# Linear attention and SwiGLU on one core: block 0's loads and order of work, and the shape of k by v

## The chip, the cores and the metric

The kernel runs on 1 core of one Trainium2 chip. The metric is the device time of one execution in microseconds (us), lower is better. Times are medians of several executions; one more execution was taken with the hardware profiler, and all rows of the profile are of that one.

## The reference

Two layers, one after the other, in float32 (the weights arrive as 64-bit words and are rounded in the kernel):

```python
kv  = einsum('bhsd,bhse->bhde', k, v)          # 8 batches, 8 heads, 576 positions, 64 wide
out = einsum('bhsd,bhde->bhse', q, kv)
rms = sqrt(mean(out * out, axis=-1, keepdims=True) + 1e-06)
x   = (out / rms * g_norm)                     # then (B,H,S,D) -> (B*S, H*D) = (4608, 512)

g   = x @ w_gate                               # 512 -> 1536
val = x @ w_val
y   = (g * sigmoid(g) * val) @ w_out           # 1536 -> 512
```

## The kernel before

The 4608 tokens are cut into 9 blocks of 512 (`BLK`), which don't coincide with the 8 batches of 576 positions. For every block n there is an `Att(n)` (attention, which yields the block's x, turned so that features lie on the partitions) and an `Ffn(n)` (the three weight products). `Att(n)` also makes the 64 by 64 matrices kv of batch n for all 8 heads, so block n needs kv of batches n - 1 and n. The later blocks' FFN uses a Strassen-like scheme with fewer products (`Up`, `Inner`, `Down`); while TensorE works on block n's FFN, attention of block n + 1 is fitted in between.

Block 0 is different: nothing runs beside it, and its FFN (`plain_up`, L956 to L961) goes through the 12 chunks f of 128 hidden features plainly, because the weights are just being loaded and rounded. Per weight piece (`Words`, 36 pieces: gate and value of each chunk, then the output weights) there is one DMA on SP (L135), two ScalarE (ACT) operations (L144 the low word, L146 the absolute value of the high word), and four VectorE (DVE) operations: L147 clamps, L152 takes the sign, L153 shifts and joins, L157 adds into the weight tile. Four load buffers (pool `ld`) go round, which the q tiles of block 0 use first.

The start of the kernel, as the code has it:

- `load_q(0)` (L268, SP): q tiles 0 and 1 of 128 positions, in pieces of 256 bytes.
- `load_kv(0)`, `load_kv(1)` (L229): per pair of heads j the 576 positions are shared out between the two halves of the partitions, 5 positions per partition (64 partitions by 5 = 320) in one and 4 (256) in the other, and the halves change places from pair to pair. That makes 8 DMAs for k (SP) and, in block 0 alone, 8 for v on ACT's queue, each on 64 partitions, 128 or 160 KB.
- `load_q(1)`: q tiles 2 and 3; `load_weights(4)`: the first four weight pieces.
- `first()`: `turn_q(0)` transposes q tiles 0 and 1 on TensorE (L307) into PSUM; the copies back go to DVE for tile 0 (L311) and ACT for the others (L309). `kv(0)`, `kv(1)` (L286) multiply k by v with 64 rows of contraction, for both halves of the partitions into two PSUM banks, which are then added: ACT copies one (L292), DVE adds the other (L111). `half(0)` is product 0 (L327, q by kv for tiles 0, 1), squares on ACT (L338), sums on DVE (L339), `root` (L345 to L357: eleven small DVE operations, a reciprocal square root by three Newton steps) and `scale` (L113). `turn_q(1)` and `product(1)` follow, and `turn_x(0)` transposes the first half of x (L374); ACT copies it back with the gain (L375).
- The main part then rounds the first two pieces, does chunk 0 for the first half of the tokens, and `second()`: root, scale and transposing of the second half. From chunk 2 on the products take all 512 tokens at once.

`tc.issue_after(ins)` orders what is traced under it behind `ins` on `ins`'s own engine; between engines only data (and buffers coming free) make one wait for another. Engines run their instructions in order, and each queue issues its DMAs in order.

In later blocks `load_kv` and `kv` work as above with all loads on SP: `kv(0)` after a third of the up products, `kv(1)` after two thirds; block 1's are done in the gap behind `plain_up`.

Of the kernel before, what the change touches and what calls it, by code (L numbers as in the profile page):

```python
# [14 lines left out]
P = 128  # L15
# [3 lines left out]
def kernel(  # L19
# [51 lines left out]
    NS = DM // P  # L71
    NF = FF // P
    NP = NF // 2
    KT = 5
    LD = 2 * (2 * KT - 1) * D
    eps = 1e-6
    assert NT == B * S and NT == NB * BLK and NB == B + 1 and S - BLK == BLK // B
    assert 2 * D == P and H == 2 * NS and (2 * KT - 1) * D == S and NS == 4

    def pool(name, bufs, **kw):  # L80
        return ctx.enter_context(tc.tile_pool(name=name, bufs=bufs, **kw))
# [37 lines left out]
    class Words:  # L119
# [12 lines left out]
        def __init__(self, src, shape):  # L132
            self.raw = ld_pool.tile([P, LD], U32, name="ld")[:, 0 : 2 * BLK]
            dst = self.raw.rearrange("p (a b) -> p a b", a=shape[0])
            self.sent = nc.sync.dma_start(out=dst, in_=src)  # L135
            self.shape = shape

        def round_to(self, dst):
            halves = self.raw.rearrange("p (f w) -> p f w", w=2)
            low, high = halves[:, :, 0], halves[:, :, 1]  # L140
            room = ring()

            unit = room[:, 0]
            nc.scalar.activation(out=unit, in_=low, func=ACT.Copy, scale=2.0**-51, bias=2.0)  # L144
            mag = room[:, 1].bitcast(U32)
            nc.scalar.activation(out=mag.bitcast(F32), in_=high.bitcast(F32), func=ACT.Abs)  # L146
            nc.vector.tensor_scalar(  # L147
                out=mag.bitcast(F32), in0=mag.bitcast(F32), scalar1=self.LOW, scalar2=self.HIGH,
                op0=OP.max, op1=OP.min,
            )  # L150
            sign = room[:, 2].bitcast(U32)
            nc.vector.tensor_scalar(out=sign, in0=high, scalar1=0x80000000, scalar2=None, op0=OP.bitwise_and)  # L152
            nc.vector.scalar_tensor_tensor(  # L153
                out=mag, in0=mag, scalar=3, in1=sign, op0=OP.logical_shift_left, op1=OP.bitwise_xor
            )
            a, b = self.shape[0], BLK // self.shape[0]
            nc.vector.tensor_tensor(  # L157
                out=dst.bitcast(U32),
                in0=mag.rearrange("p (a b) -> p a b", a=a, b=b),
                in1=unit.bitcast(U32).rearrange("p (a b) -> p a b", a=a, b=b),  # L160
                op=OP.add,
            )
# [15 lines left out]
    def round_w(name, j):  # L178
        if name == "o":
            dst = wo[:, j : j + 1, :]  # L180
        else:
            dst = wviews[name][0][j // 2][:, :, P * (j % 2) : P * (j % 2 + 1)]
        words.pop((name, j)).round_to(dst)

    class Att:

# [18 lines left out]

        def place_kv(self, g, i):

            n = (2 * g + i) * LD
            if self.n == 0:
                return self.room.rearrange("p f t -> p (f t)")[:, n : n + LD]  # L210
            if self.n == 1 and g == 0:
                return self.room[:, n : n + LD]
            return ld_pool.tile([P, LD], F32, name="ld")

        def load_kv(self, g):


            if self.n == B:
                return
            for i, (views, src) in enumerate(((self.k, k), (self.v, v))):  # L220
                tile_ = self.place_kv(g, i)
                for e in range(2):
                    j, s0 = 2 * g + e, 0
                    for r in range(2):
                        m = KT - (r != e)
                        at = 2 * D * (KT - r) * e
                        t = tile_[r * D : (r + 1) * D, at : at + 2 * D * m].rearrange("p (h x) -> p h x", h=2)
                        queue = nc.scalar if self.n == 0 and i else nc.sync
                        queue.dma_start(  # L229
                            out=t,  # L230
                            in_=src[self.n, 2 * j : 2 * j + 2, s0 : s0 + m * D].rearrange("h (p t) d -> p h (t d)", t=m),
                        )
                        views[j, r] = t.rearrange("p h (t d) -> p h t d", t=m)
                        s0 += m * D

        def load_quarters(self, i):

# [35 lines left out]
        def kv(self, g):  # L273


            if self.n == B:
                return
            if g == 0:
                self.kv_ps = [m_psum.tile([P, NS, D], F32, name="m") for _ in range(2)]
            for e in range(2):  # L280
                j = 2 * g + e
                for c in range(KT):
                    for r in range(2):
                        m = KT - (r != e)
                        for u in range(2 if c < m else 0):
                            nc.tensor.matmul(  # L286
                                self.kv_ps[r][u * D : (u + 1) * D, j, :], lhsT=self.k[j, r][:, u, c, :],
                                rhs=self.v[j, r][:, u, c, :], start=(c == 0), stop=(c == m - 1),
                            )
            if g == 1:  # L290
                dst = kvs[self.n % 3]
                nc.scalar.copy(out=dst, in_=self.kv_ps[0])  # L292
                self.kv_made = add(nc.vector, dst, self.kv_ps[1], dst)

        def turn_q(self, i, pools=None):

            if i == 0:
                self.qt = ring().rearrange("p j (t c) -> p t j c", t=T)
            if self.n >= TURNED:
                to = self.qt[:, :, 2 * i : 2 * i + 2].rearrange("p t j c -> p j t c")  # L300
                nc.vector.transpose(out=to.rearrange("p j t c -> p (j t c)"), in_=self.q[i])
                return
            for t in (2 * i, 2 * i + 1):
                pool = pools[t % 2] if pools else m_psum
                ps = pool.tile([P, NS, P], F32, name=pool.name[0])
                for j in range(NS):
                    nc.tensor.transpose(ps[:, j], self.q[t][:, j], ident)  # L307
                if t:
                    nc.scalar.copy(out=self.qt[:, t], in_=ps)  # L309
                else:  # L310
                    nc.vector.tensor_copy(out=self.qt[:, t], in_=ps)  # L311

        def product(self, i, pools=None):
# [7 lines left out]
            for t in range(2):  # L321
                for j in range(NS):
                    for b, _, p0, p1 in self.parts(2 * i + t):
                        for p in range(p0, p1, D):
                            for u in range(2):
                                rows = slice(u * D, (u + 1) * D)
                                nc.tensor.matmul(  # L327
                                    self.ps[i][u][p : p + D, t, j, :],
                                    lhsT=self.qt[rows, 2 * i + t, j, p : p + D], rhs=kvs[b % 3][rows, j, :],
                                    start=True, stop=True,  # L330
                                )
# [4 lines left out]
            for u in range(2):  # L336
                sq = self.sq[:, 2 * i + u]
                self.squared = nc.scalar.activation(out=sq, in_=self.ps[i][u], func=ACT.Square)  # L338
                nc.vector.tensor_reduce(out=self.z[:, i, u], in_=sq, axis=mybir.AxisListType.X, op=OP.add)  # L339

        def root(self, i, k=1):

# [84 lines left out]

        def first(self):
            self.turn_q(0, (b_psum, c_psum))
            for g in range(2):  # L430
                self.kv(g)
            self.half(0)
            squared = self.squared
            self.turn_q(1, (b_psum, c_psum))
            with tc.issue_after(self.scaled.ins):
                self.product(1, (b_psum, a_psum))
            self.turn_x(0)
            return squared, self.scaled

        def second(self):  # L440
            self.root(1)
            self.scale(1)
            self.turn_x(1)
            return self.scaled

        def turn(self):
            for i in range(2):
# [548 lines left out]
    blocks = [Att(n) for n in range(NB)]  # L996
    blocks[0].room = h_pool.tile([P, NF, BLK], F32, name="h")
    blocks[0].load_q(0)
    for g in range(2):
        blocks[0].load_kv(g)  # L1000
    blocks[0].load_q(1)
    load_weights(4)
    squared, scaled = blocks[0].first()
# [1 line left out]
    for n in range(NB):  # L1005
        ffn = Ffn(n, blocks[n])
        nxt = blocks[n + 1] if n + 1 < NB else None
        if n == 0:
# [1 line left out]
            with tc.issue_after(squared.ins), tc.issue_after(scaled.ins):  # L1010
                weights(2)
            ffn.plain_up(0, (0,))
            scaled = blocks[0].second()
            for f in range(NF):
                with tc.issue_after(scaled.ins), tc.issue_after(blocks[0].copied.ins) if f else ExitStack():
                    weights(2 * (f + 2))
                if f == 1:
                    ffn.plain_up(1, (0,))
                    ffn.plain_up(0, (1,))
                ffn.plain_up(f, (1,)) if f == 1 else ffn.plain_up(f) if f else None  # L1020
            weights(len(pieces))
            pairs = wo.rearrange("p (j e) d -> p e j d", e=2)
            t2(pairs[:, 0, :, HD:DM], pairs[:, 1, :, HD:DM], pairs[:, 0, :, 0:HD])
# [22 lines left out]
            ffn.up({4: third, 8: two_thirds} if nxt else {})  # L1046
        if nxt:
            nxt.turn()
        if n + 2 < NB:
            blocks[n + 2].load_kv(0)  # L1050
        if TURNED - 2 <= n < NB - 2:
            ffn.loads = blocks[n + 2].load_q
# [2 lines left out]
                    ffn.loads(i)  # L1055
        ffn.down(nxt)
        if n == 0:

            with tc.issue_after(nxt.halves[0].ins):
                for j in range(NP):  # L1060
# [32 lines left out]
```

## Time and profile before

| | |
|---|---|
| median of 5 runs | 1040.93 us (1039.65 to 1041.39) |
| the profiled execution | 1041.1 us, span in the profile 1039.3 us, mean granted clock 0.995 |
| L956, all of block 0's up product on TensorE | busy 36.0 + 36.0 + 9.8 + 7.8 us |
| L286, k by v of block 0 | 144 passes, median 311 ns; 936 of later blocks from the load buffers, median 218 ns |
| first and last L286 pass of block 0 | 7.81 and 16.3 us |
| DVE, in the stretch 80 to 109 us | busy 28.5 of 29 us |

The span is cut into rows of operations with their engine, line, tile, shape and time; start times are us from the span's start. A matmul of float32 appears as two passes, each with a load of its weights (PEld). "Idle before" names what ended an engine's wait. SPq and ACTq are the queues that issue DMAs; a DMA's issue is short, its landing comes 2 to 8 us later. POOL is GpSimd. Busy time of TensorE says that it has work, not that its clock is at full rate: that is the granted clock, a column of the tables of windows.

### The profile page before, as it was taken

What the parts mean: (1) busy time and instruction counts of PE and PEld (TensorE: products, weight loads), DVE (VectorE), ACT (ScalarE), POOL (GpSimd) and SP (SyncE); (2) the same over time, 40 slices, a digit from 0 to 9 for tenths busy, and PEclk for the clock granted to TensorE, in tenths of its full rate; (3) what the DMA queues carried; (4) which work ended last, traced back from release to release, by engine and by line L of the source; (5) the groups of instructions that cost most, each with busy time, mean ns of one, the idle gap of its engine ahead of it and who ended that gap; (6) DMA issues with size and microseconds to landing.
All of it is one profiled execution on the core that took longest, in us unless ns stands there. A gap on an engine that the chain in (4) does not pass through costs nothing.

```text
span 1039.3 us, 21544 instructions
## 1 busy us (share of the span) xinstructions
PE 1011.5 (97%) x8588; PEld 907.5 (87%) x8588; DVE 700.2 (67%) x1202; ACT 232.0 (22%) x357; POOL 368.9 (35%) x280
## 2 busy tenths in 40 slices
PE   4899999999999999999999999999999999999998
PEld 3644688778899989998999899988999899989997
DVE  2999596888656866675666666684668566856661
ACT  3666111222212111121111111211122111212110
POOL 0000443435024631563147305640455136512670
PEclk9899999999999999999999999999999999999999
DMA  9689604665457556764676377726862666066611
GB/s 213 189 257 274 151 1 126 186 196 142 129 179 242 134 108 196 242 161 82 196 239 190 60 203 229 218 48 172 249 194 52 162 207 188 29 153 210 191 31 41
DMA packets 255044, 168.16 MB, mean 162 GB/s; under 512 B 124640, under 2 KB 230240, under 8 KB 254944
## 3 DMA queue, kind: packets, MB, share of 16 engines
q1 hardware_dynamic: 228384, 162.45, 55.7%
q10 hardware_dynamic: 26496, 4.33, 2.4%
q8 instruction: 68, 1.11, 0.4%
q14 instruction: 32, 0.26, 0.1%
q0 software_dynamic: 64, 0.00, 0.0%
HBM read 138.02 MB, written 22.41 MB: 154 GB/s over the span
## 4 chain that ended last, share of the span: by engine, by line
PE 91%; DVE 4%; DMA 3%; issue 1%; ACT 1%; POOL 0%; SPq 0%; DVEq 0%; ACTq 0%; POOLq 0%
PE b L662 25%; PE b L513 20%; PE c L662 12%; PE c L513 9%; PE a L662 6%; PE a L513 5%; PE b L956 4%; PE c L956 4%; PE m L286 1%; PE m L327 1%; DVE xi L112 1%; DMA w<-t 1%; DVE r L111 1%; DVE r L112 1%; DMA h<-in_k_dram 1%
## 5 line engine op out<-in xcount | busy, mean ns | idle before, releaser
L111 POOL TENSOR_TENSOR r<-r 128x256 f32<-128x256 f32 (+1 forms) x105 | 110.8, 1061 | 308.9 <-DVE r L111 233.3
L111 DVE TENSOR_TENSOR r<-b,r 128x512 f32<-128x512 f32 (+1 forms) x273 | 161.9, 606 | 64.0 <-PE b L662 58.9
L112 POOL TENSOR_TENSOR t<-wo 128x512 f32<-128x512 f32 x81 | 115.2, 1447 | 195.4 <-DVE wo L111 106.7
L111 DVE TENSOR_TENSOR r<-c,r 128x512 f32<-128x512 f32 (+1 forms) x179 | 108.5, 618 | 88.9 <-PE c L662 49.5
L662 PE MATMUL b<-x,t 128*128 128x128 f32 x1092 | 151.0, 275 | 0.0
L662 PEld LDWEIGHTS b<-x,t 128*128 128x128 f32 x1092 | 136.5, 192 | 0.6 <-DVE r L111 0.2
L111 DVE TENSOR_TENSOR r<-a,r 128x512 f32<-128x512 f32 (+1 forms) x99 | 62.5, 631 | 110.3 <-PE a L513 65.8
L113 POOL TENSOR_TENSOR h<-r 128x1024 f32<-128x1024 f32 (+1 forms) x40 | 81.5, 2053 | 88.0 <-DVE r L111 73.7
L662 PE MATMUL c<-xi,t 128*128 128x128 f32 x840 | 112.2, 275 | 0.3 <-DVE xi L111 0.3
L662 PEld LDWEIGHTS c<-xi,t 128*128 128x128 f32 x840 | 102.8, 192 | 0.4 <-DVE xi L111 0.4
L513 PE MATMUL b<-wo,h 128*128 128x256 f32 x432 | 99.4, 382 | 0.1
L513 PE MATMUL b<-t,h 128*128 128x256 f32 x432 | 96.9, 381 | 0.0
L513 PEld LDWEIGHTS b<-t,h 128*128 128x128 f32 x432 | 81.3, 190 | 11.3 <-issue 0.2
L513 PEld LDWEIGHTS b<-wo,h 128*128 128x128 f32 x432 | 79.9, 190 | 12.7 <-DVE h L113 2.5
L676 ACT COPY r<-b 128x512 f32<-128x512 f32 x63 | 36.9, 586 | 212.7 <-PE b L662 205.9
L662 PE MATMUL b<-xi,t 128*128 128x128 f32 x588 | 79.7, 276 | 0.0
L662 PEld LDWEIGHTS b<-xi,t 128*128 128x128 f32 x588 | 72.4, 192 | 0.0
L662 PE MATMUL b<-x,wg 128*128 128x128 f32 x336 | 52.7, 279 | 0.2 <-DVE x L112 0.2
L662 PE MATMUL b<-x,wv 128*128 128x128 f32 x336 | 51.3, 275 | 0.0
L956 PE MATMUL b<-x,wg 128*128 128x512 f32 (+1 forms) x112 | 45.8, 552 | 3.5 <-ACT r L144 2.4
L513 PE MATMUL c<-t,s 128*128 128x256 f32 x216 | 48.3, 380 | 0.0
L513 PE MATMUL a<-wo,h 128*128 128x256 f32 x216 | 48.3, 379 | 0.0
(133 smaller groups left out, 1582.8 us busy)
## 6 DMA issues: line engine op xcount, KB each, us to landing
t<-w SPq DMA_DIRECT2D x336, 256.0 KB, 3.4
out_dram<-r SPq DMA_DIRECT2D x17, 512.0 KB, 3.1
ld<-in_moe_w_gate_dram SPq DMA_DIRECT2D x12, 512.0 KB, 4.7
ld<-in_moe_w_val_dram SPq DMA_DIRECT2D x12, 512.0 KB, 4.8
ld<-in_moe_w_out_dram SPq DMA_DIRECT2D x12, 512.0 KB, 4.6
w<-t SPq DMA_DIRECT2D x18, 256.0 KB, 2.5
w<-xi SPq DMA_DIRECT2D x12, 384.0 KB, 3.1
ld<-in_k_dram SPq DMA_DIRECT2D x26, 160.0 KB, 3.9
```

Of the source, the lines that this page charges most:

```text
L111: add = lambda e, o, a, b: e.tensor_tensor(out=o, in0=a, in1=b, op=OP.add)
L112: sub = lambda e, o, a, b: e.tensor_tensor(out=o, in0=a, in1=b, op=OP.subtract)
L113: mul = lambda e, o, a, b: e.tensor_tensor(out=o, in0=a, in1=b, op=OP.mult)
L286: nc.tensor.matmul(self.kv_ps[r][u * D : (u + 1) * D, j, :], lhsT=self.k[j, r][:, u, c, :], rhs=self.v[j, r][:, u, c, :], start=(c == 0), ...
L327: nc.tensor.matmul(self.ps[i][u][p : p + D, t, j, :], lhsT=self.qt[rows, 2 * i + t, j, p : p + D], rhs=kvs[b % 3][rows, j, :], start=True, ...
L513: nc.tensor.matmul(banks[e][:, e], lhsT=lhsT, rhs=rhs, start=first and i == 0 and (e == 0 or banks[0] is not banks[1]), stop=i == self.ste ...
L662: nc.tensor.matmul(ps[:, i, f], lhsT=self.weight(o, p, f), rhs=self.operand(o, p), start=first and (i, f) == (0, 0), stop=True, skip_group ...
L676: nc.scalar.copy(out=dst, in_=ps)
L956: nc.tensor.matmul(t, lhsT=w[f // 2][:, i, P * (f % 2) : P * (f % 2 + 1)], rhs=x[:, i, of], start=(i == 0), stop=(i == NS - 1),)
```

## The change

Block 0:

- k and v of positions 0 to 511 are loaded as 4 positions by 128 partitions, 4 heads to a DMA (512 KB, all on SP); the last 64 positions come in four small DMAs on ACT's queue, onto the half of the partitions that their heads use. `first_kv` multiplies them: per head 4 chunks for each half of the partitions and one chunk of the last 64 positions, 72 products as before.
- `first()` has another order: product 0 stands ahead of turning q tiles 2 and 3; their copies go to DVE (tile 2) and ACT (tile 3).
- Rounding of a weight piece is cut into `begin` (absolute value; the three DVE operations) and `finish` (low word; the last add). The first piece's `begin` stands between the sums of the first and the second half; the second half's squares and sums come behind it.
- One `root` serves both halves (twice as wide), then come the first half's scaling, the first piece's `finish`, the second half's scaling.
- `warm()`: seven products of 512 columns with the identity, whose output nobody reads, stand on TensorE behind product 1 and in front of transposing x.
- Chunk 1 is no longer cut into halves.

Later blocks: k and v of a pair of heads lie on one half of the partitions, 9 positions to a partition (64 by 9 = 576), 288 KB per DMA, half as many DMAs. Each PSUM bank then holds finished matrices for its heads; ACT copies the two banks, and DVE's add is gone. Block 2's first load is traced behind the down product of block 0 instead of ahead of it.

```diff
-        def round_to(self, dst):
+        def begin(self):
+            self.begun = True
...
+        def finish(self, dst):
+            unit = self.room[:, 0]
+            nc.scalar.activation(out=unit, in_=self.low, func=ACT.Copy, scale=2.0**-51, bias=2.0)
...
+        def load_first_kv(self):
+            room = self.room.rearrange("p f (h x) -> p (f h) x", h=2)
+            most = {"k": room[:, 0:H], "v": room[:, H : 2 * H]}
+            last = {x: room[:, 2 * H + i].rearrange("p (h d) -> p h d", d=D) for i, x in enumerate("kv")}
+            for g in range(2):
+                heads, rows = slice(NS * g, NS * (g + 1)), slice(D * g, D * (g + 1))
+                for x, src in (("k", k), ("v", v)):
+                    nc.sync.dma_start(
+                        out=most[x][:, heads], in_=src[0, heads, 0:BLK].rearrange("h (p t) d -> p h (t d)", t=T)
+                    )
+                    nc.scalar.dma_start(out=last[x][rows], in_=src[0, heads, BLK:S].rearrange("h p d -> p h d"))
...
+        def first_kv(self):
+            banks = [m_psum.tile([P, NS, D], F32, name="m") for _ in range(2)]
+            for j in range(NS):
+                g = j // 2
+                for c in range(T + 1):
+                    for r in range(2) if c < T else (g,):
+                        for u in range(2):
...
+            nc.scalar.copy(out=kvs[0], in_=banks[0])
+            add(nc.vector, kvs[0], banks[1], kvs[0])
...
-                for e in range(2):
-                    j, s0 = 2 * g + e, 0
-                    for r in range(2):
-                        m = KT - (r != e)
...
+                for r in range(2):
+                    j = 2 * g + r
+                    t = tile_[r * D : (r + 1) * D].rearrange("p (h x) -> p h x", h=2)
+                    nc.sync.dma_start(
+                        out=t, in_=src[self.n, 2 * j : 2 * j + 2].rearrange("h (p t) d -> p h (t d)", t=KT)
+                    )
...
             if g == 1:
-                dst = kvs[self.n % 3]
-                nc.scalar.copy(out=dst, in_=self.kv_ps[0])
-                self.kv_made = add(nc.vector, dst, self.kv_ps[1], dst)
+                dst = kvs[self.n % 3].rearrange("p (g r) d -> p r g d", r=2)
+                for r in range(2):
+                    nc.scalar.copy(out=dst[:, r], in_=self.kv_ps[r])
...
         def first(self):
             self.turn_q(0, (b_psum, c_psum))
-            for g in range(2):
-                self.kv(g)
-            self.half(0)
-            squared = self.squared
-            self.turn_q(1, (b_psum, c_psum))
-            with tc.issue_after(self.scaled.ins):
+            self.first_kv()
+            self.product(0)
+            with tc.issue_after(self.multiplied.ins):
+                self.turn_q(1, (b_psum, c_psum))
+            with tc.issue_after(self.copied_q.ins), tc.issue_after(self.summed.ins):
+                begun = words[pieces[0]].begin()
+            with tc.issue_after(begun.ins):
                 self.product(1, (b_psum, a_psum))
+            self.warm()
+            self.root(0, 2)
+            self.scale(0)
+            with tc.issue_after(self.squared.ins), tc.issue_after(self.scaled.ins):
+                weights(1)
             self.turn_x(0)
-            return squared, self.scaled
-
-        def second(self):
-            self.root(1)
             self.scale(1)
-            self.turn_x(1)
-            return self.scaled
+            return self.squared, self.scaled
+
+        def warm(self):
+            ps = c_psum.tile([P, NS, P], F32, name="c")
+            for _ in range(7):
+                nc.tensor.matmul(ps, lhsT=ident, rhs=self.qt[:, 3], start=True, stop=True)
...
-                if f == 1:
-                    ffn.plain_up(1, (0,))
-                    ffn.plain_up(0, (1,))
-                ffn.plain_up(f, (1,)) if f == 1 else ffn.plain_up(f) if f else None
+                ffn.plain_up(f) if f else ffn.plain_up(0, (1,))
```

## The prediction

> **What bounds the kernel now.** I read four views: the page's engine shares, TensorE's waits, a table of windows, and the timeline of the first 50 us.
>
> ```profile
> PE 1011.5 (97%) x8588; PEld 907.5 (87%) x8588; DVE 700.2 (67%) x1202; ACT 232.0 (22%) x357; POOL 368.9 (35%) x280
> ```
>
> ```profile
> PE m L286 <- DMA h<-in_k_dram: 9.7, 2, 7.8
> PE m L374 <- DVE r L113: 3.1, 1, 3.1
> PE b L956 <- ACT r L144: 2.4, 1, 2.4
> PE m L327 <- issue: 1.2, 1, 1.2
> ```
>
> TensorE (PE) is the bound at 97%. What it waits for (us in total, times, longest) lies nearly all in block 0, so a gain is an earlier start of its unbroken stream.
>
> ```profile
> 7.50:10.00 2.50, 0.87 (x10) 0.71 (x10) 0.00 (x0) 0.71 (x1) 0.00 (x0) 1.00 1.13 232
> 14.00:16.00 2.00, 2.00 (x94) 2.00 (x91) 0.00 (x0) 0.18 (x1) 0.00 (x0) 1.00 1.29 214
> 18.00:20.00 2.00, 0.84 (x37) 0.64 (x27) 0.69 (x1) 0.68 (x3) 0.00 (x0) 1.00 1.08 348
> 26.00:28.00 2.00, 0.42 (x2) 0.02 (x1) 2.00 (x7) 1.93 (x4) 0.00 (x0) 0.50 0.01 4
> 30.00:32.00 2.00, 2.00 (x7) 1.55 (x6) 1.68 (x11) 0.68 (x1) 0.00 (x0) 0.50 0.75 227
> 47.00:60.00 13.00, 13.00 (x32) 5.80 (x32) 12.43 (x27) 8.59 (x15) 0.00 (x0) 1.00 0.80 248
> ```
>
> Columns: stretch, its length, busy us of PE, weight load, DVE, ACT, POOL, then granted clock, DMA share, GB/s. Three rates matter: 232 GB/s while k and v come (64 partitions), 214 while the last q comes (256-byte packets), 348 while weights come (128 partitions, 1 KB packets). The clock is halved after PE's idle time, and from 47 on PE is never idle.
>
> ```profile
> 13.49 2.99 PE L286 MATMUL m<-h 64*64 64x64 f32 x114
> 17.33 1.02 PEld L327 LDWEIGHTS m<-kv,r 64*64 64x64 f32 x63 [0.17 <-DVE kv L111]
> 23.67 1.29 DVE L113 TENSOR_TENSOR r<-m,y 128x512 f32<-128x512 f32 x2
> 28.83 3.75 PE L956 MATMUL b<-x,wg 128*128 128x256 f32 x8 [2.41 <-ACT r L144]
> 32.38 1.94 PE L956 MATMUL c<-x,wv 128*128 128x256 f32 x8
> 37.43 1.99 PE L956 MATMUL b<-x,wg 128*128 128x256 f32 x8 [0.77 <-DVE wg L157]
> 47.03 3.60 PE L956 MATMUL b<-x,wg 128*128 128x512 f32 x8
> ```
>
> Two milestones: the first half's scaling (L113) ends at 24.96, and chunk 2 of the up product starts at 47.03. Between lie 22.07 us, of which chunks 0 and 1 need 13.7 (32 passes of 0.43, from the last row). The same 8 passes of 256 columns take 3.75 us at the low clock and 1.9 later.
>
> **The change, part by part.**
>
> *Loads of block 0.* Sixteen DMAs (eight k on SP, eight v on ACT) become four of 512 KB on 128 partitions (SP) and four of 64 KB in 256-byte packets (ACT). DMAs in flight share completion slots: in the trace SP's third k issue waits until ACT's first v has landed (4.90 us, issue at 4.92). In the changed kernel as built the second big k waits so for ACT's first small load; behind it on SP stand the second v, both late q and the weights. By 5.0 us 715 kB have come; at 232 GB/s that means a start at 1.9. Then q 0, 1 and the small loads, 786 kB at 214, take 3.7 us; the first big k and v, 1.05 MB at 348, 3.0 (8.6); the second pair 3.0 (11.6); q 2 1.2 (12.8), q 3 1.2 (14.0), first weights 1.5 (15.5). The upper bound for k, v is 232 GB/s, putting the second pair at 14.6. I take 348, the row with the same partitions and packet size. A 64 KB load and one q before the slot-waiting DMAs are within the first 786 kB, so they should be down near 5, while the first big pair still feeds the engines.
>
> The page "DMA: Bandwidth & Descriptors" of the Trainium skill (Why small descriptors are slow) counts about 3 bus cycles per packet beside one per 32 bytes: 8 of 11 useful at 256 bytes, 32 of 35 at 1 KB, so 0.80 of the speed. The rows give 214 against 348, 0.61; by the page the 786 kB would take 2.8 us instead of 3.7 and the forecast would be 0.9 lower; I keep the rows.
>
> *k by v on TensorE.* The 144 passes stay. L286 ran one per 26 ns (2.99 us by 114), L327 one per 16. The 72 passes of the second pair, after idle time, at 26: 1.9, to 13.5. From the end of these products (16.48) to the first of L327 were 0.85 us, ACT's copy and DVE's add, both kept: the first product starts at 14.35.
>
> *The order up to the scaling.* PE now does product 0 before it turns q 2 and q 3. Its 64 passes cost 1.0 at 16 ns (to 15.55 with the last's latency) or 1.7 at 26. Turning q 2 is 0.66 (1.11 as at 11.59, cold); its copy goes to DVE (0.6, L311's 0.69 less overlap) and stands there ahead of the sums, so a late q 2 holds all of DVE. Then on DVE two sums of L339 1.2, the first weights' three operations (26.06 to 27.4 in the trace: 1.27), two sums of the second half 1.2, one root for both halves (eleven operations, 2.3 as at 21.30 to 23.58; twice the width, between nothing and 1.9 if time doubled with it; I take 0.2), scaling 1.29. The weights' ACT half and the four squares, 0.6 each, run beside and finish first (18.0 and 19.3). Sum from 15.55, warm: 0.66 + 0.6 + 1.2 + 1.27 + 1.2 + 2.5 + 1.3 = 8.7, with waits 24.4. Cold: 25.5. I take 25.0 against 24.96 before: the earlier data pay for the work put in front.
>
> *What no longer lies behind the scaling.* Before, DVE did the second sums (1.27), the two first pieces, then a second root (2.9) and scaling (1.3), idled 1.03, and only then the next two pieces. Now, with S the scaling's end: weights finished 0.6, second scaling 1.2, second piece with two operations of the third in between 2.6: value weights ready at S + 4.45. PE: turning 0.5, ACT's x copy 0.65, gate half (8 by 0.215) over at S + 2.8; value half S + 4.45 to 6.15. ACT: two copies to S + 1.85, three weight steps 1.7, table load 1.28, Silu 0.35, one step 0.6, second half's copies from S + 5.85. PE: second half from S + 6.5, 3.44, over at S + 9.95; its weights are ready at S + 8.75. Chunk 1, 6.87: chunk 2 starts at S + 16.9. Its own pieces are done at S + 14.7 and 16.2, needed at 16.9 and 20.3. With S = 25.0 that is 41.9, and 47.03 - 41.9 = 5.1 us gained.
>
> *The filler.* Seven matmuls of 512 columns, 14 passes of 0.43, 6.0 us, stand on PE in front of turning x. After product 1 (17.4 to 18.0) they end at 24.0, before S = 24.4: hidden. In the cold case they start near 20 and end at 26.0, 0.5 after S. The reader sees why they are there: from 21.9 to 25.0 PE is idle and the clock is 0.50 from about 25.6 to 32.5; without them about 2.1 of the 5.1 would go (3.75 + 1.94 - 3.6).
>
> The page "TensorE: Matmul & The Clock Gate" (The HAM clock gate) speaks against a fixed filler: its 3.4 us window is free-running, so how many passes are slow varies from run to run. The low-clock stretch of 6.9 us is two such windows, which agrees; by the page an unlucky phase leaves up to 3.4 us at half rate, some 1.7 us lost, and the forecast would be that much higher at worst.
>
> *Behind 47 us.* DVE's rounding (nearly full from 26 to 109) moves up by the work that now precedes S, 6 to 7 us, so it stays ahead; POOL's first subtractions of the output weights (109.52) start right behind it; and the last multiply waits for PE (DVE idle 5.95 before 115.97). The shift is kept. *Later blocks:* the add (0.42, eight times) goes off DVE and ACT's 0.37 copy becomes two of, by the rows 0.37 for 256 and 0.59 for 512 columns, about 0.27; hidden by the 5.35 us of the first down product (119.98) between copy and use; uncovered, eight times 0.17, 1.4 us. Half as many loads of 128/160 KB become 288 KB, each 0.6 of SP; PE's waits for DMA behind 47 us are 0.5 in all, the most that this can gain. Loss bound from both, 1.4; I take nothing.
>
> The sum goes against the profiled execution: 1041.1 us, span 1039.3, 0.2 over the median 1040.93. 1041.1 - 5.1 = **1036.0**.
>
> **Rivals.**
> *Slow start:* k, v come at 232 as before, or instruction fetch stalls PE 1.16 us again (the "issue" wait in L327, at about the same count of instructions, which is now the turning of q 2), or the filler runs partly cold. For it: these rows were all measured here; against it: 128-partition rows at 348. Gain 5.1 - 3.0 = 2.1: 1039.0; the stall alone 1037.2.
> *Fast start:* PE is warm throughout and both pairs overlap; second products at 16 ns (0.75 less), S at 23.6: gain 6.5, 1034.6.
> *Hidden anyway:* rounding, not PE, paces 47 to 109, where DVE is 12.43 of 13 busy; then the gain is only what DVE gains after stalls, near 0 to 1: 1040.5. Against it: PE waits for no DVE there, and needs 6.87 per chunk against DVE's 4.4.
> *Slower:* q 2 late in front of DVE's sums. Each us that it lands after about 15 is a us of S. From 8.75 us behind its landing S follows; the gain is gone when S passes 30.1, landing at 21.4, or 160 GB/s over the first 3.1 MB. At 150: 22.9, S 31.6, chunk 2 at 48.5, 1042.6. No window of half a microsecond between 14 and 20 us shows under 190.
>
> **How the numbers follow.** Forecast (1034.8 to 1037.6) 0.66; slow start (to 1039.4) 0.18; fast 0.09; hidden 0.04; slower 0.03. The likeliest gives 1036.0. The range 1033.9 to 1038.9 takes in fast and nearly all of slow start. 0.2% is 2.1 us, about what this kernel's measurement can tell from no change: faster than 1038.85 is the forecast, fast, and two thirds of slow start, 0.87; same is the rest of it and hidden, 0.10; slower 0.03.
>
> **What would show it.** Second big v landed near 11.6; scaling of half 0 ending at 24 to 26; no clock below 1.00 after the filler's first passes; gate half in 1.9 us rather than 3.75; the first pass of chunk 2 near 42; unbroken PE behind it. I am wrong if S is past 27, if PE stalls for weights between chunks 1 and 3, or if PE loses time in later blocks at k by v.

## The result and the profile after

The changed kernel takes 1038.11 us (median of 28 runs, 1037.04 to 1039.5) against 1040.73 of the kernel before beside it (48 runs, 1039.32 to 1042.03): a ratio of 0.9976, interval 0.9971 to 0.9981. It is 2.6 us faster where 5.1 were forecast. The profiled execution took 1039.47 us, the upper end of its runs, so single times of this trace may lie a microsecond later than in a typical run.

TensorE's longest waits up to 130 us, changed kernel (engine, line, what it waited for: us in total, times, longest):

```profile
PE m L247 <- DMA h<-in_v_dram: 5.8, 2, 4.9
PE b L337 <- DMA ld<-in_q_dram: 4.2, 1, 4.2
PE m L357 <- DVE kv L111: 0.6, 1, 0.6
```

The 9.7 us for k, the 3.1 in front of transposing x and the 2.4 for the first weights are gone or have become waits for q and v. Yet the work that follows did not move up. The timeline of the same execution (start, length, operation; TensorE, then the two scalings of DVE's first half in one row):

```profile
4.18 1.09 PE L337 MATMUL b<-ident,ld 128*128 128x128 f32 x4 [4.18 <-DMA ld<-in_q_dram]
11.78 2.40 PE L247 MATMUL m<-h 64*64 64x64 f32 x72 [4.90 <-DMA h<-in_v_dram]
15.05 2.42 PE L247 MATMUL m<-h 64*64 64x64 f32 x72 [0.88 <-DMA h<-in_v_dram]
18.07 1.98 PE L357 MATMUL m<-kv,r 64*64 64x64 f32 x64 [0.60 <-DVE kv L111]
19.99 1.11 PE L337 MATMUL b<-ident,ld 128*128 128x128 f32 x4
23.58 6.28 PE L482 MATMUL c<-r,ident 128*128 128x512 f32 x14
29.79 1.07 PE L404 MATMUL m<-ident,r 128*128 128x128 f32 x8
31.20 1.99 PE L994 MATMUL b<-x,wg 128*128 128x256 f32 x8 [0.34 <-ACT x L405]
46.78 3.60 PE L994 MATMUL b<-x,wg 128*128 128x512 f32 x8
28.36 1.29 DVE L113 TENSOR_TENSOR r<-m,y 128x512 f32<-128x512 f32 x2
```

Read it from the data on. TensorE begins on the first pair of k and v at 11.78, where the forecast had it down at 8.6, and on the second at 15.05, not 11.6. Its 72 passes take 2.42 us (34 ns each, before 26), product 0 takes 1.98, turning q 2 1.11: TensorE is at half rate. The filler (L482) runs from 23.58 to 29.86 and the scaling ends at 29.65. Transposing x (L404) starts 0.14 behind that, as it does in e2 below (28.26 and 28.40), whose filler ends earlier: the filler holds nothing up. The gate half takes 1.99 instead of 3.75. Chunk 2 starts at 46.78, only 0.25 ahead of before.

The windows (stretch, length, busy PE, weight load, DVE, ACT, POOL, granted clock, DMA share, GB/s):

```profile
7.50:10.00 2.50, 0.00 (x0) 0.00 (x0) 0.00 (x0) 0.00 (x1) 0.00 (x0) 1.00 1.12 318
12.00:14.00 2.00, 2.00 (x72) 1.99 (x68) 0.00 (x0) 0.00 (x0) 0.00 (x0) 1.00 1.25 274
14.00:16.00 2.00, 1.12 (x40) 0.98 (x40) 0.00 (x0) 0.00 (x0) 0.00 (x0) 1.00 0.72 150
30.00:32.00 2.00, 1.66 (x12) 1.34 (x11) 2.00 (x5) 1.54 (x3) 0.00 (x0) 1.00 0.00 0
```

The rate while k and v come is 318, near the 348 I took, but it is 150 in the window in which the second pair is completed. The granted clock reads 1.00 throughout, also in 12 to 14, where a pass takes twice its later time: this early, the column does not show the half rate. From 30 on, where the kernel before had 0.50, it is 1.00 in truth as well.

Two milestones place each kernel below: S, the end of the first half's scaling, and the start of chunk 2. What is left of the profiled time behind chunk 2 was 994.07 before (1041.1 - 47.03) and is 992.69 now (1039.47 - 46.78). So in this pair of executions 0.25 us came from block 0 and 1.4 from later work. One pair says little: among the profiles below, kernels with the same code behind chunk 2 take 991.3 us (e5, e6) to 994.0 (e10) there, and why is not shown.

### The profile page after: what moved, and what is told of

It reads as the page before. It is cut to its first block, busy times and chain, and to the rows that moved or that the text cites. A ratio compares the mean times of both kernels' runs of the same rounds, so it can differ in the third digit from the quotient of the medians.

```text
span 1037.7 us, 21446 instructions
## 1 busy us (share of the span) xinstructions
PE 1016.1 (98%) x8586; PEld 906.5 (87%) x8586; DVE 700.0 (67%) x1184; ACT 231.3 (22%) x362; POOL 369.3 (36%) x280
## 3 DMA queue, kind: packets, MB, share of 16 engines
q8 instruction: 68, 1.11, 0.4%
## 4 chain that ended last, share of the span: by engine, by line
PE 91%; DVE 4%; DMA 2%; issue 1%; ACT 1%; SPq 0%; POOL 0%; DVEq 0%; ACTq 0%; POOLq 0%
PE b L700 25%; PE b L551 20%; PE c L700 12%; PE c L551 9%; PE a L700 6%; PE a L551 5%; PE b L994 4%; PE c L994 4%; PE m L316 2%; PE m L357 1%; DVE xi L112 1%; DMA h<-in_v_dram 1%; DVE r L112 1%; PE c L482 1%; DMA t<-w 1%
## 5 line engine op out<-in xcount | busy, mean ns | idle before, releaser
L551 PE MATMUL c<-wo,h 128*128 128x256 f32 x216 | 48.1, 379 | 0.0
```

Source lines behind the costliest of these rows:

```text
L551: nc.tensor.matmul(banks[e][:, e], lhsT=lhsT, rhs=rhs, start=first and i == 0 and (e == 0 or banks[0] is not banks[1]), stop=i == self.ste ...
```

## The experiments

All times are medians; a ratio is to runs of the kernel before taken beside them, whose own median went from 1040.56 to 1041.28. So differences between kernels of different groups carry some 0.7 us, and the ratios decide. My first theory (A) was that both halves of the change contribute. The rivals named cold TensorE (C), load sharing (E), the size of loads (L), the place of q's transposes (O) and instruction fetch (G).

**The two halves apart.** One kernel takes only the later blocks' loads and k by v, the other all but these.

```diff
# e1: the kernel before, with
+            if self.n:
+                self.kv9(g)
# e2: the changed kernel, its load_kv and kv for blocks 1 to 8 as before (m = 5 - (r != e))
```

> The kernel before, with only the later blocks' k by v changed to 9 positions (loads, products, two ACT copies). Theory A (the later blocks gave most of the measured gain: the two traces stand 0.25 us apart at the start of chunk 2 and 1.7 us apart at the end): 1.2 to 2.0 us faster than before, the difference arising in block 1 (span 160 to 245), with the kernel's start unchanged. Theory B (the later blocks are hidden, the difference in block 1 is chance of that stage, and the gain is block 0's): within 0.5 us of before.

> The changed kernel with the later blocks' k by v put back to 5 and 4 positions. Theory A: only 0.5 to 1.2 us faster than before, chunk 2 starting near 46.8. Theory B: 2.2 to 2.8 us faster, as the whole change. If the parts add up, this gain and that of the later blocks alone sum to 2.6.

Later blocks alone: 1039.24 against 1041.01, ratio 0.9985 (0.9976 to 0.9994), 1.6 us. Block 0 alone: 1039.62, ratio 0.9986 (0.9978 to 0.9995), 1.4 us, between what the two theories had. Together 3.0 against the 2.6 measured, so the halves add up within their intervals, and "I take nothing" for the later blocks was wrong. Where the gain of the later blocks comes from is not shown. The 936 passes of their k by v occupy 18.3 us of TensorE in the changed kernel instead of 19.2, but that is not seen as time: from the first store of block 1 to the end of the span the profiles take 756.2 us before, 756.0 in e1 and 756.2 in the changed kernel. The difference lies between the first stores of blocks 0 and 1, 126.47 us apart before, 125.36 in e1 and 125.20 in the changed kernel. There TensorE waits for ScalarE's r (4.7 to 6.2 us in all), and its clock dips in some profiles (mean 0.99 from 157 to 283 us before and in the changed kernel, 1.00 in e1), which does not go with the gain. Among the profiles of all kernels with the new later blocks that stretch runs from 124.78 to 127.43, so one profile each does not settle what shortened it.

**The filler taken out (e3).**

```diff
-            self.warm()
```

> The changed kernel without the seven matmuls on the identity (their output is read by nobody). If the filler only holds the clock: the matmul passes behind the first scaling run at half rate again for one or two clock windows, chunk 2 starts 1.5 to 3 us later, time 1.5 to 3 us above the changed kernel, that is 0 to 1 us slower or equal to before. If the filler stands in the way (it ends at 29.86, 0.2 us after the scaling's end at 29.65): the transposes start 0.2 us earlier and the time is the same or up to 0.3 us lower.

1040.14, ratio 0.9992 (0.9984 to 1.0001): by the medians 2.0 us slower than with the seven products that nobody reads.

```profile
28.19 1.94 PE L404 MATMUL m<-ident,r 128*128 128x128 f32 x8 [6.33 <-DVE r L113]
30.05 2.69 PE L993 MATMUL b<-x,wg 128*128 128x256 f32 x8
```

TensorE is idle 6.33 us before the transposes, these take 1.94 instead of 1.07, the gate half 2.69 instead of 1.99, and S to chunk 2 18.1 us instead of 17.1. That 1.0 is what this trace shows of the filler's worth. Another 1.1 lies behind chunk 2 (993.80 against 992.69), where the code is the same.

**TensorE kept warm while k and v load**, first with large fillers (e4: 3 and 1 products of 512 columns ahead of the two groups), then with small ones (e7: 12 and 4 of 128 columns, whose edit is shown).

```diff
             for j in range(NS):
                 g = j // 2
+                if j % 2 == 0:
+                    self.idle((12, 4)[g])
```

> The changed kernel with filler matmuls also while k and v are on the way: three before the first group of k by v, one before the second (output read by nobody). Theory C (TensorE's low clock up to 23.5 us is 2.5 us of the late scaling): the second group's 72 passes take 1.2 us instead of 2.4, product 0 1.0 instead of 2.0, turning 0.5 instead of 1.0; the scaling ends near 27, chunk 2 starts 1.5 to 2.8 us earlier, time 1.5 to 2.8 us below the changed kernel. Theory D (loads alone set it; the passes are slow for another reason, such as data still landing): passes stay at 31 to 34 ns, and the time is the same or up to 1 us higher.

> As the kernel with fillers while k and v are on the way, but in 16 matmuls of 128 columns instead of 4 of 512 (32 passes instead of 8, about the same time). There TensorE stood 2.7 us in product 0 for instructions, at its 221st pass, while the weights came at over 320 GB/s. Theory G (the next block of instructions is fetched at a fixed count of instructions and queues behind the loads; reached 24 passes earlier, it is fetched before the weights come): no 'issue' wait over 0.5 us in product 0, clock 1.00 throughout, scaling ends near 27, time 1.5 to 2.8 us below the changed kernel. Theory H (the stall has another cause): it stays at 1 to 3 us, time within 1 us of the changed kernel.

Large: 1038.83, ratio 0.9979 (0.9971 to 0.9988), no gain over the changed kernel, and a wide spread (1036.54 to 1041.14). Small: 1036.57, ratio 0.9962 (0.995 to 0.9975), 1.5 faster than it. The timeline with the large ones, of the slowest of its twelve runs:

```profile
15.45 1.40 PE L249 MATMUL m<-h 64*64 64x64 f32 x72 [0.89 <-DMA h<-in_v_dram]
21.45 0.45 PE L359 MATMUL m<-kv,r 64*64 64x64 f32 x3 [2.73 <-issue]
```

The first row shows what the cold TensorE had cost: 72 passes take 1.40 where the changed kernel needs 2.42, at the same clock reading. The second shows what ate the gain in this execution: near the end of product 0 TensorE stands 2.73 us and waits for nothing that the profile names. With the small fillers there is no such pause; S is 26.71 and chunk 2 starts at 43.83, 1.55 ahead of e2, which has the same loads without these fillers.

**The late q kept out of the loads' way (e5)**: q 2 and q 3 are issued only once the last v has landed.

```diff
+                    if self.n == 0 and i == 1:
+                        tc.add_manual_dep(sent.ins, self.big.ins.name, ...)
```

> The changed kernel with q tiles 2 and 3 issued only once the second big v has landed (the weights stand behind them on SP). Theory E (loads in flight share the DMA engines, so the second pair of k and v is slowed by the q loads issued after it): the second v lands 1.5 to 2.5 us earlier (near 12.5 instead of 13.4 to 15.0), q 2 near 15.5 and still ahead of its use, the first half's scaling ends 1.5 to 2 us earlier, time 1.0 to 2.0 us below the changed kernel. Theory F (loads land in the order of issue, at the rate of their packets): the second v lands as before, q 2 two us later, time the same or up to 1 us higher.

1036.98, ratio 0.9967 (0.9954 to 0.9979). The second v lands at 13.91, as in e2 (13.93) and later than in e3 (13.44), which both still have q behind them: the sharing with q is not what made it late. With no q or weights in flight the last bytes still trickle in:

```profile
10.00:12.00 2.00, 1.00 (x37) 1.03 (x41) 0.00 (x0) 0.00 (x0) 0.00 (x0) 1.00 1.06 329
12.00:14.00 2.00, 1.48 (x51) 1.32 (x47) 0.00 (x0) 0.00 (x0) 0.00 (x0) 1.00 0.19 62
```

Share 0.19 and 62 GB/s for the 1.9 us before the landing: a load of 512 KB has a tail during which most of the path is free. S is 28.46 here. By the ratios the total is 0.9 better than the changed kernel's, with intervals that overlap, and block 0, as late as in e2, shows no reason for it.

**Finer loads (e6)**: four pairs of 256 KB, two heads each, instead of two of 512 KB.

```diff
-                for x, src in (("k", k), ("v", v)):
+                for e in range(2):
+                    two = slice(NS * g + 2 * e, NS * g + 2 * e + 2)
+                    for x, src in (("k", k), ("v", v)):
...
-                        out=most[x][:, heads], in_=src[0, heads, 0:BLK].rearrange(...)
+                        out=most[x][:, two], in_=src[0, two, 0:BLK].rearrange(...)
```

> The changed kernel with the big k and v loads cut into four pairs of 256 KB (two heads each) instead of two pairs of 512 KB. If what counts is the TensorE work behind the last landing: 36 passes instead of 72 stand there, 1.2 us less at the low clock, time 0.5 to 1.2 us below the changed kernel. If the waits for completion slots count (six of the eight now wait for another load to land): the last v lands 1 us or more later, time 0 to 2 us higher.

1033.89 (1033.66 to 1034.26), ratio 0.9935 (0.9922 to 0.9949): 6.7 us faster than before, 4.2 than the changed kernel. Its timeline:

```profile
8.36 0.91 PE L250 MATMUL m<-h 64*64 64x64 f32 x22 [8.36 <-DMA h<-in_v_dram]
9.20 1.11 PE L340 MATMUL b<-ident,ld 128*128 128x128 f32 x4
11.10 3.51 PE L250 MATMUL m<-h 64*64 64x64 f32 x122
15.40 1.16 PE L360 MATMUL m<-kv,r 64*64 64x64 f32 x64 [0.79 <-DVE kv L111]
42.57 3.60 PE L997 MATMUL b<-x,wg 128*128 128x512 f32 x8
```

k by v ends at 14.6 instead of 17.5, product 0 takes 1.16, S is 25.45 and chunk 2 starts at 42.57: nearly the forecast's 25.0 and 41.9. But the rows show a second difference beside the size of the loads. The scheduler has put the transposes of q 0 and q 1 (L340 at 9.20) between the first 22 and the other 122 passes, as in the kernel before, whereas the changed kernel has them ahead of all passes. So TensorE has no pause from 8.36 to the end of k by v.

**Size and order apart.** Finer loads with the transposes held ahead (e8); the same with small fillers in the pauses (e9); and the changed kernel with block 0's loads and pass order of before (e10).

```diff
# e8: as e6, and
-            self.first_kv()
+            with tc.issue_after(self.turned.ins):
+                self.first_kv()
# e9: as e8, and ahead of each pair
+                self.idle((5, 2, 2, 2)[j])
# e10: the changed kernel, and
-    blocks[0].load_first_kv()
+    for g in range(2):
+        blocks[0].load_split(g)
```

> The kernel with four pairs of 256 KB (1033.89 us) differed from the changed kernel in two things: the size of the loads, and, because the scheduler placed them there, the transposes of q 0 and q 1 between the first 22 and the other 122 passes of k by v, which kept TensorE busy from 8.4 us on. Here the loads stay fine and the transposes stand ahead of k by v again, as in the changed kernel. Theory L (the size of the loads): k by v still ends at 14.3 to 14.9 in place of 17.5, the first half's scaling ends at 25 to 26, and the time is 1033.5 to 1034.8. Theory O (the order, TensorE kept busy): with pauses between the pairs the passes run at 33 ns to the end, k by v ends past 15.5, product 0 takes 1.9 to 2.0 and the turning of q 2 1.1, the scaling ends past 27 and the time is 1035.5 to 1037.5.

> As the run beside it, with small products of 128 columns (5 ahead of the first pair, 2 ahead of each later one) on TensorE while it waits for k and v; nobody reads their output. If the cold TensorE still costs something with the fine loads: the 36 passes of the last pair take 0.6 to 0.8 instead of 1.2, k by v ends at 13.9 to 14.3, the scaling at 24.3 to 25.2, time 1032.8 to 1033.6. If it costs nothing any more, because the passes of the first pairs warm it: as the run beside it within 0.4. If the fillers get in the way of the landed data: 0.5 to 1 slower than it.

> The changed kernel with block 0's loads of k and v, and the order of their passes, as in the kernel before (sixteen loads on 64 partitions, v on ACT's queue; the transposes of q 0 and q 1 behind the first 30 passes), everything else as changed: rounding in between, one root, filler, later blocks. Theory of the forecast (the new shape of the loads buys 3 us of earlier data): slower than the changed kernel by 1 to 3, 1039 to 1041. Theory of the runs so far (two pairs of 512 KB bring the data no earlier than before, and leave TensorE cold): k by v ends at 16.3 to 16.8 as before against 17.5, the scaling at 26.3 to 27.5, 1035.5 to 1037.0; with a stall for instructions of some 1.2 in product 0 or the turning of q 2, as before, 1036.5 to 1038.2.

Transposes ahead: 1037.27, ratio 0.9958 (0.9945 to 0.9972). With fillers: 1035.95, 0.9951 (0.9937 to 0.9964). Loads as before: 1036.93, 0.9962 (0.9948 to 0.9976). The first of them:

```profile
8.71 1.33 PE L250 MATMUL m<-h 64*64 64x64 f32 x36 [1.81 <-DMA h<-in_v_dram]
10.25 1.33 PE L250 MATMUL m<-h 64*64 64x64 f32 x36 [0.21 <-DMA h<-in_v_dram]
11.77 1.34 PE L250 MATMUL m<-h 64*64 64x64 f32 x36 [0.18 <-DMA h<-in_v_dram]
13.31 1.34 PE L250 MATMUL m<-h 64*64 64x64 f32 x36 [0.20 <-DMA h<-in_v_dram]
15.35 1.99 PE L360 MATMUL m<-kv,r 64*64 64x64 f32 x64 [0.69 <-DVE kv L111]
18.88 1.11 PE L340 MATMUL c<-ident,ld 128*128 128x128 f32 x4 [0.49 <-issue]
21.84 7.42 PE L486 MATMUL c<-r,ident 128*128 128x512 f32 x14
```

Both theories hold in part. The pairs land 1.53 us apart (524 kB each, 343 GB/s, the rate of the forecast) and k by v ends at 14.65 as with the other order: that is the size of the loads. But four pauses of a fifth of a microsecond leave TensorE cold to the end: 37 ns a pass, product 0 1.99, and the filler, late and partly cold, ends at 29.26, 1.57 behind S (27.69). S is 2.24 later than in e6 and S to chunk 2 1.2 longer (18.3), together 3.46, with equal loads. In that stands the wait of 0.49 in the last row but one, of which more below. This execution is the slowest of e8's five (1035.6 to 1037.86); all five are slower than every run of e6, by 3.4 us in the medians and 2.4 by the ratios.

With fillers the passes of the later pairs take 0.8 and S is 26.09, yet the median is 2.1 above e6's, more than any of the three cases had. The profiled run, the fastest of the five (1034.82), has a wait of 0.27 without a name in product 0 (it ends at 16.66). The 2.1 stay unexplained in size.

With the loads of before k by v ends at 16.97, product 0 takes 1.16 and S is 28.40, in a profile of the slowest of five runs (1039.48): by the medians the changed kernel's new loads, in its order, lose about 1.2 us to the old ones in theirs, but the two intervals overlap, so what is shown is that the new loads do not win. They were the step that was to bring product 0 forward by 3 (from 17.33 to 14.35).

**The order alone, and a warm start.** e11 moves only the transposes of q 0 and q 1 in the changed kernel behind 36 passes; e12 does so with fine loads and puts 14 products of the identity ahead of all.

```diff
# e11: the changed kernel, and
-            self.turn_q(0, (b_psum, c_psum))
             self.first_kv()
...
+                if j == 1:
+                    with tc.issue_after(made.ins):
+                        self.turn_q(0, (b_psum, c_psum))
# e12: e6 with the same, and ahead of it
+            for _ in range(14):
+                made = nc.tensor.matmul(ps[:, 0], lhsT=ident, rhs=ident, start=True, stop=True)
```

> The changed kernel, loads as they are (two pairs of 512 KB), with only the place of the transposes of q 0 and q 1 on TensorE moved: behind the first 36 of the 144 passes of k by v (as the scheduler had put them, behind 22 and 30, in the kernel with fine loads and in the one with the loads of before) instead of ahead of all. Theory O (a TensorE that has no pause from the first pair on is warm when the last data land): k by v ends where it did, 17.2 to 17.8, product 0 takes 1.1 to 1.3 instead of 1.98 and the turning of q 2 0.66 instead of 1.11, the first half's scaling ends at 27.8 to 28.6 instead of 29.65, time 1036.4 to 1037.2. If the order did nothing: within 0.4 of the changed kernel's 1038.1. If the transposes, now behind the first pair's landing, hold up the second pair's products: k by v ends at 18.3 or later, 1038.5 to 1039.5.

> The kernel with four pairs of 256 KB and the transposes of q 0 and q 1 behind the first 36 passes, and 14 small products of the identity with itself ahead of all (about 2.9 to 7.8 us; nobody reads them), so that TensorE is warm when the first pair lands near 8.4. If the cold start still costs it something: k by v ends at 13.9 to 14.3 in place of 14.6 (bound by the last pair's landing near 13.3), the scaling at 24.7 to 25.1 instead of 25.45, time 1033.0 to 1033.6. If fetching instructions behind the loads decides (as a pause of 0.3 to 2.7 us in product 0 or the turning of q 2 in the kernels with more instructions ahead of it): a pause there, and 1034.2 to 1036.

e11: 1039.58 (1036.98 to 1041.1), ratio 0.9979 (0.997 to 0.9987), no faster than the changed kernel (0.3 slower by the ratios, 1.5 by the medians) where I expected 1.3 faster. e12: 1036.73, 0.9957 (0.9945 to 0.9969), 2.8 slower than e6 by the medians. The timeline of e11, then that of e12:

```profile
18.12 1.16 PE L366 MATMUL m<-kv,r 64*64 64x64 f32 x64 [0.75 <-DVE kv L111]
19.21 0.66 PE L346 MATMUL b<-ident,ld 128*128 128x128 f32 x4
22.77 0.90 PE L346 MATMUL c<-ident,ld 128*128 128x128 f32 x3 [2.79 <-issue]
```

```profile
15.09 0.81 PE L372 MATMUL m<-kv,r 64*64 64x64 f32 x40 [0.79 <-DVE kv L111]
17.37 0.92 PE L372 MATMUL m<-kv,r 64*64 64x64 f32 x24 [1.47 <-issue]
18.21 1.12 PE L352 MATMUL b<-ident,ld 128*128 128x128 f32 x4
```

In both the warm half of the theory came true: product 0 in 1.16 and turning in 0.66 in e11, 20 ns a pass in e12. Then comes the wait that the profile puts down to nothing but issue, and behind it TensorE is cold again (turning 1.12 in e12, clock 0.50 in 24 to 26 in e11). S is 31.36 and 27.90.

The DMA queues point to what that wait is. Beside those for data there is one for instructions; in the stretch 20 to 21 us of e11 (packets, MB, share of 16 engines):

```profile
q8 instruction: 1, 0.02, 6.6%
```

One packet of some 16 KB, about 1 us long (6.6% of 16 engines for 1 us). Counting the passes in each timeline, the wait always falls behind 219 to 221 passes, wherever that is in the program: in product 0 with many fillers, among the transposes without. Set side by side (us; the packet's start to 0.2):

| kernel | packet starts | pass 220 reached | wait | TensorE goes on | from packet's start |
|---|---|---|---|---|---|
| fine loads (e6) | 14.2 | 17.1 | none | | |
| fine, warm start (e12) | 14.6 | 15.9 | 1.47 | 17.37 | 2.8 |
| small fillers (e7) | 14.6 | 17.0 | none | | |
| fine, fillers (e9) | 14.0 | 16.4 | 0.27 | 16.66 | 2.7 |
| fine, q first (e8) | 16.6 | 18.4 | 0.49 | 18.88 | 2.3 |
| loads as before (e10) | 17.0 | 19.3 | 0.44 | 19.78 | 2.8 |
| later blocks alone (e1) | 16.6 | 18.7 | 1.02 | 19.68 | 3.1 |
| kernel before | 17.0 | 18.5 | 1.16 | 19.64 | 2.6 |
| changed kernel | 17.8 | 21.0 | none | | |
| large fillers (e4) | 19.0 | 18.7 | 2.73 | 21.45 | 2.5 |
| q between (e11) | 20.0 | 20.0 | 2.79 | 22.77 | 2.8 |

Work goes on 2.3 to 3.1 us after the packet's start; a kernel that reaches pass 220 sooner waits for the difference. No row speaks against it, nor do e2, e3 and e5, which reach pass 220 2.8 to 4.2 us behind the packet's start and don't wait. It is a reading of traces all the same: no run moves the packet alone. What decides when the packet gets its turn, between 14.0 and 20.0, stays open: fine loads in two orders have it at 14.2 and 16.6. That it waits behind the loads, which run at 240 to 370 GB/s in most of those microseconds, is only argued.

## Why the prediction was half right

*Behind S.* Forecast 16.9 us to chunk 2; 17.1 in the changed kernel and in e2, e4, e5, e6, e7, e9, e10 and e12, however early or late S was. The reordered rounding, the joint root, the uncut chunk 1 and the filler did what the sum said. It is longer where the filler ended 0.69 and 1.57 behind S (17.5 in e11, 18.3 in e8) and where it was missing (18.1 in e3). Without the filler the forecast lost 2.1; e3's trace shows 1.0 of it here, and what made up the rest of the 2.0 between the medians is not shown.

*S itself* is the step that failed: "I take 25.0", measured 29.65 in the profile, and 28.26 and 28.04 in e2 and e3 with the same loads. The forecast's own sign of being wrong, S past 27, came true. Product 0 was to start at 14.35 and starts at 18.07, 3.72 late: the second pair lands 3.45 late (15.05 against 11.6), its passes take 0.52 more (34 ns against 26), and the joining is 0.25 quicker. From product 0 to S the forecast had 10.65, of which 0.6 for a partly cold TensorE, and the trace has 11.58. Warm, in e6, this chain takes 10.05, as the sum's warm case had it; of the 1.53 between the two, product 0 and the turning at half rate are 1.27.

*"I take 348, the row with the same partitions and packet size."* The rate was near (318 and 332 from 7.5 to 12 us of this trace) and the conclusion wrong, because I turned bytes over rate into landings one after the other. Of the 3.45 us 3.18 stand already at the first pair (11.78 against 8.6; 10.83 and 10.35 in e2 and e3), and from there to the second are 3.27 against 3.0. By 11.6 us 2.5 MB had come (219 GB/s from the start), while q 0, q 1, the small loads and the first pair are 1.84 MB: loads issued behind the first pair came beside it. In e5, without q in flight, the second pair still lands at 13.91 behind 1.9 us at 62 GB/s. The 72 passes then all stand behind the last landing. Only the upper bound I gave, 14.6, was near. (The k issue that waits until 4.92 in the trace before is SP's second, not its third; no term rests on that.)

*Cold passes.* I took 26 ns for the second group, product 0 at 1.0 to 1.7, and "cold" as a case 0.5 us above the 25.0. I had read that rate from the kernel before, where the transposes lie between the groups; that the change puts them ahead, and so opens a pause of 4.9 us on TensorE, stood in the changed program's order and I did not price it. The page "TensorE: Matmul & The Clock Gate" of the Trainium skill (The HAM clock gate) has the array at half rate by default, until it has been busy for a window of about 3.4 us; the 34 and 37 ns against 16 to 20 agree, and e8 shows that short pauses are enough to keep it there.

*The instruction stall* was in my slow rival at 1.16 us, "at about the same count of instructions". The count was right; its price runs from nothing to 2.79, and a quicker TensorE raises it. In the changed kernel half rate and late data hid it: with the packet at 17.8 a warm TensorE would have reached pass 220 some 1.3 earlier, at 19.7, and stood until 20.1 to 20.9 (an estimate from the table). In e7 the packet came at 14.6 and there was no wait. Its gain of 1.5 is S 1.55 earlier than in e2: 1.0 from the second group's passes, 0.55 from product 0 and 0.45 from the turning, less 0.35 for a later landing and 0.13 for a slower joining.

*Later blocks:* the sum took 0 with bounds of a loss of 1.4 and a gain of 0.5; e1 measured a gain of 1.6 (0.6 to 2.5). Which term was missing stays open; the runs place the gain in block 1's stretch, not its cause.

So the total, 2.1 us above the point and inside the range, is two misses that partly cancel: block 0 gave 1.4 of 5.1, later blocks 1.6 of 0. To that extent the total was luck. By its time the result looks like the slow-start rival; its mechanism is a cold TensorE, in my sum a case of 0.5, together with loads that land late beside each other, not the 232 GB/s.

## What to carry to other kernels

At a kernel's start, split the first loads so that work can begin on the first quarter and little stands behind the last, and place independent work between the groups that wait for data, not ahead of them: both together were worth 4.2 us here (1038.11 to 1033.89), more than the whole change. Neither did it alone: the finer loads in the old order gained 0.8 by the medians and 1.9 by the ratios, with intervals that just overlap (e8), and the order with large loads gained nothing, and in its profile TensorE stood 2.79 us for instructions (e11). A program's order as scheduled belongs into the forecast, because a pause decides at what rate everything behind it runs. Every pass put ahead makes TensorE reach the end of its block of instructions sooner, so a filler is priced by where the count of passes then stands, too.

## What the runs showed of the hardware

- By the table above TensorE stops at about its 220th pass until a block of instructions is there, for 0.27 to 2.79 us in eight of the profiles; 2.3 to 3.1 us lie between the fetch's start and the next pass.
- The granted clock reads 1.00 in the first 20 us whether a pass takes 16 or 37 ns; the durations of like passes show the cold TensorE there.
- The page "DMA: Bandwidth & Descriptors" of the Trainium skill (Bandwidth) advises loads of at least 1 MiB for bandwidth. No load here is that large, and between the sizes here the rate hardly differs: from 10 to 12 us it is 344 GB/s with two pairs of 512 KB (e2, e3; 332 in the changed kernel) and with four of 256 KB (e8). The landings differ: the last 512 KB had 1.9 us at 62 GB/s ahead of its landing (e5), and TensorE began at 8.71 with the small loads (e8) and at 10.35 (e3) to 12.00 (e11) with the large ones.
- Issuing a load can itself take microseconds while others are in flight: in the changed kernel the two late q kept SP's queue for 4.91 us, with fine loads (e6) for 1.15.
